# Folding two weight matrices on chip, normalising attention in transposed layout and writing out the order of every engine: linear attention and a multiplicative FFN on one core

## The chip, the cores and the metric

The kernel runs on one core of a Trainium2 chip. A core has five engines with queues of their own: TensorE (PE, with its weight loads PEld), VectorE (DVE), ScalarE (ACT), GpSimd (POOL) and SyncE (SP, which issues the transfers). The metric is device time in microseconds, the median of several runs.

## The reference

```python
def _attn_ref(q, k, v):                      # each (8, 8, 576, 64), f32
    phi = lambda x: np.where(x > 0, x, np.exp(x) - 1.0) + 1.0
    q_p, k_p = phi(q), phi(k)
    kv = np.einsum('bhsd,bhse->bhde', k_p, v)
    z = np.sum(k_p, axis=2)
    num = np.einsum('bhsd,bhde->bhse', q_p, kv)
    den = np.einsum('bhsd,bhd->bhs', q_p, z)[..., None] + 1e-06
    return num / den

def _moe_ref(x, w1, w2, w3, w_out):          # x (4608, 512); w1, w2 (512, 1024)
    a = x @ w1                               # w3 (1024, 1024); w_out (1024, 512)
    b = x @ w2
    h = a * b @ w3                           # (a * b) @ w3
    return h @ w_out

# x is the attention's output, heads side by side: 8 batches x 576 tokens, 8 heads x 64
```

## The kernel before

Two parts share one program. The attention part takes one batch at a time (`attn_load_b`, then `attn_for_b`); the FFN part takes chunks of 512 tokens (`moe_for_chunk`, 9 chunks).

`attn_load_b` loads k, v and q in tiles of 128 tokens (five a batch, the last of 64), all from SP's queue; a tile's piece in memory is 64 floats, 256 bytes. `phi` makes max(x + 1, exp(min(x, 0))) in four steps: two on VectorE from f32 (L80, L82), an Exp on ScalarE (L81), a max on VectorE (L83). v is copied with a column of ones beside each head, so that one product gives both k'v and the sum of k'.

`attn_for_b` forms that product for two heads at a time (kvp, L127), copies its two useful blocks into kvc, and then, for each tile of tokens, transposes q by a matmul with the identity (trp, L146), copies it out (qpT, L153), multiplies by kvc (np, L159), divides in token-major layout on VectorE (L169, L172, L178), transposes the result back (tr, L182) and copies it into xt (L188), the transposed activations of all 4608 tokens.

`moe_for_chunk` forms, for each of eight feature blocks f, a and b (8 matmuls of 512 columns, L201 and L208), copies a out on ScalarE (L215) and multiplies by b on VectorE (L216). Then comes h: for each of eight blocks 8 matmuls with w3 (L222) and a cast on VectorE (L228). Then the output: for each 128 tokens 8 matmuls with w_out (L234), a copy on ScalarE (L241) and a store of 256 KB (L242). A chunk has 64 + 64 + 32 long matmuls.

All weights are loaded by `load_weights`, after the first batch's attention, in 24 pieces through three buffers, each cast to bf16 on VectorE (L59). The source loops over batches, issues the loads of the next batch ahead, and takes an FFN chunk as soon as its tokens are there. The order in which each engine gets its instructions is set by the planner of the language, which weaves attention and FFN work together.

## Time and profile before

| | |
|---|---|
| time, median of 3 runs (range) | 420.39 us (420.13 to 421.15) |
| span of the profiled execution | 417.6 us |
| its own time | not listed apart; the span is 2.8 us under the median |
| TensorE busy | 373.7 us, 89% |
| VectorE busy | 240.5 us, 58% |
| ScalarE busy | 182.0 us, 44% |
| read from and written to memory | 38.8 MB and 9.4 MB |
| granted TensorE clock, mean | 1.000 |

The span runs from the first to the last instruction. The page has the busy time of each engine, the span in 40 slices of 10.4 us with the busy share in tenths, the queues, the chain of work that ended last, and groups of instructions (count, busy time, mean duration in ns, and the idle time just before them). A timeline lists instructions in order: start, length, engine, line, shape, count; in brackets the idle time before and what ended it. A matmul's listed length holds its way through the pipeline, so that what one costs in a row is the distance between starts. Stretches give, for each interval: length, then busy time of PE, PEld, DVE, ACT and POOL with counts, the granted clock, the mean share of the queues and GB/s.

### The profile page before, as it was taken

What the parts mean: (1) busy time and instruction counts of PE and PEld (TensorE: products, weight loads), DVE (VectorE), ACT (ScalarE), POOL (GpSimd) and SP (SyncE); (2) the same over time, 40 slices, a digit from 0 to 9 for tenths busy, and PEclk for the clock granted to TensorE, in tenths of its full rate; (3) what the DMA queues carried; (4) which work ended last, traced back from release to release, by engine and by line L of the source; (5) the groups of instructions that cost most, each with busy time, mean ns of one, the idle gap of its engine ahead of it and who ended that gap; (6) DMA issues with size and microseconds to landing.
All of it is one profiled execution on the core that took longest, in us unless ns stands there. A gap on an engine that the chain in (4) does not pass through costs nothing.

```text
span 417.6 us, 5799 instructions
## 1 busy us (share of the span) xinstructions
PE 373.7 (89%) x2042; PEld 178.1 (43%) x2080; DVE 240.5 (58%) x696; ACT 182.0 (44%) x373; POOL 0.7 (0%) x6
## 2 busy tenths in 40 slices
PE   1054699899999999999999999999999999999996
PEld 0032344344444544454445444544454444444442
DVE  4667678776796698668947871353135313331440
ACT  4565543157755783678348701640164013103202
POOL 0000000000000000000000000000000000000000
PEclk9999999999999999999999999999999999999999
DMA  9998288996993998399639001100110011002002
GB/s 180 201 216 232 80 301 278 260 230 152 187 179 86 224 212 149 86 220 210 116 89 230 14 11 52 48 2 0 53 49 2 0 52 51 0 11 91 2 0 100
DMA packets 121180, 48.61 MB, mean 116 GB/s; under 512 B 113472, under 2 KB 113472, under 8 KB 121152
## 3 DMA queue, kind: packets, MB, share of 16 engines
q1 hardware_dynamic: 121152, 48.25, 52.3%
q8 instruction: 16, 0.26, 0.3%
q14 instruction: 12, 0.10, 0.1%
HBM read 38.80 MB, written 9.44 MB: 115 GB/s over the span
## 4 chain that ended last, share of the span: by engine, by line
PE 77%; ACT 9%; DVE 5%; DMA 4%; SPq 3%; issue 2%; ACTq 0%; DVEq 0%
PE h_ps L222 29%; PE o_ps L234 15%; PE b_ps L208 12%; PE a_ps L201 11%; PE np L159 4%; ACT qpT L153 3%; PE kvp L127 3%; PE tr L182 2%; DMA t<-in_moe_w_dram 2%; ACT xt L188 2%; ACT tmp L81 1%; DMA qt<-in_q_dram 1%; SPq L102 1%; ACT kvc L137 1%; SPq L97 1%
## 5 line engine op out<-in xcount | busy, mean ns | idle before, releaser
L222 PE MATMUL h_ps<-ab_t,w_sb 128*128 128x512 bf16 x565 | 127.9, 379 | 1.8 <-DVE w_sb L59 1.1
L222 PEld LDWEIGHTS <-w_sb 128*128 128x128 bf16 x576 | 55.2, 98 | 66.1 <-DVE w_sb L59 2.0
L201 PE MATMUL a_ps<-xt,w_sb 128*128 128x512 bf16 x273 | 78.1, 385 | 0.4
L208 PE MATMUL b_ps<-xt,w_sb 128*128 128x512 bf16 x282 | 77.6, 380 | 0.6 <-issue 0.2
L228 DVE CAST h_t<-h_ps 128x512 bf16<-128x512 f32 x72 | 49.5, 690 | 42.0 <-PE h_ps L222 40.8
L81 ACT ACTIVATE tmp<-tmp 128x512 bf16<-128x512 bf16 (+1 forms) x80 | 50.3, 633 | 53.0 <-DVE tmp L80 52.7
L216 DVE TENSOR_TENSOR ab_t<-a_sb,b_ps 128x512 bf16<-128x512 f32 x72 | 49.1, 682 | 42.1 <-PE b_ps L208 39.5
L241 ACT COPY o_sb<-o_ps 128x512 f32<-128x512 f32 x36 | 21.1, 585 | 99.4 <-PE o_ps L234 98.8
L234 PE MATMUL o_ps<-wo_sb,h_t 128*128 128x512 bf16 x282 | 63.3, 379 | 0.3
L215 ACT COPY a_sb<-a_ps 128x512 f32<-128x512 f32 x72 | 42.4, 589 | 41.6 <-PE a_ps L201 36.1
L234 PEld LDWEIGHTS <-h_t 128*128 128x128 bf16 x288 | 28.2, 98 | 33.9 <-DVE h_t L228 0.2
L208 PEld LDWEIGHTS <-w_sb 128*128 128x128 bf16 x288 | 26.5, 97 | 26.5 <-issue 1.0
L201 PEld LDWEIGHTS <-w_sb 128*128 128x128 bf16 x288 | 26.9, 99 | 24.5 <-issue 0.8
L188 ACT CAST xt<-tr 128x512 bf16<-128x512 f32 (+1 forms) x40 | 21.7, 542 | 30.5 <-PE tr L182 30.4
L169 DVE TENSOR_SCALAR den<-np 128x4 f32<-128x4 f32 (+1 forms) x80 | 11.4, 160 | 40.7 <-PE np L159 39.9
L127 PE MATMUL kvp<-vt_all,kp_all 128*128 128x130 bf16 (+1 forms) x160 | 19.3, 242 | 17.1 <-ACT vt_all L107 17.1
L178 DVE TENSOR_TENSOR o_t<-np,den 128x256 bf16<-128x256 f32 (+1 forms) x80 | 31.6, 415 | 0.1
L182 PE MATMUL tr<-ident,o_t 128*128 128x128 bf16 (+1 forms) x160 | 22.9, 229 | 9.7 <-DVE o_t L178 9.3
L159 PE MATMUL np<-kvc,qpT 128*128 128x130 bf16 (+1 forms) x160 | 18.9, 240 | 8.5 <-ACT qpT L153 6.0
L182 PEld LDWEIGHTS <-o_t 128*128 128x128 bf16 (+1 forms) x160 | 13.2, 100 | 29.9 <-DVE o_t L178 22.2
L107 ACT CAST vt_all<-vt 128x512 bf16<-128x512 f32 (+1 forms) x40 | 24.6, 614 | 1.6 <-DMA vt<-in_v_dram 1.2
L127 PEld LDWEIGHTS <-kp_all 128*128 128x128 bf16 (+1 forms) x160 | 11.9, 103 | 25.3 <-DVE kp_all L83 17.7
(24 smaller groups left out, 205.5 us busy)
## 6 DMA issues: line engine op xcount, KB each, us to landing
out_dram<-o_sb SPq DMA_DIRECT2D x36, 256.0 KB, 2.0
kt<-in_k_dram SPq DMA_DIRECT2D x32, 256.0 KB, 5.0
vt<-in_v_dram SPq DMA_DIRECT2D x32, 256.0 KB, 5.0
qt<-in_q_dram SPq DMA_DIRECT2D x32, 256.0 KB, 5.1
t<-in_moe_w_dram SPq DMA_DIRECT2D x16, 512.0 KB, 4.6
t<-in_moe_w_out_dram SPq DMA_DIRECT2D x8, 256.0 KB, 3.1
kt<-in_k_dram SPq DMA_DIRECT2D x8, 128.0 KB, 4.8
vt<-in_v_dram SPq DMA_DIRECT2D x8, 128.0 KB, 4.4
```

The lines of the kernel that those rows point to most:

```text
L81: nc.scalar.activation(out=tmp, in_=tmp, func=AF.Exp)
L127: nc.tensor.matmul(kvp[:, a, :], kp_flat[:ssz, st, hp_ * P:(hp_ + 1) * P], vt_flat[:ssz, st, hp_ * (2 * D + 2):(hp_ + 1) * (2 * D + 2)], s ...
L159: nc.tensor.matmul(nps[hp_ // 2][:ssz, hp_ % 2, :], qpT[:, hp_, :ssz], kvc[:, hp_, :], start=(hp_ % 2 == 0), stop=(hp_ % 2 == 1),)
L178: nc.vector.tensor_tensor(out=dst, in0=num_src, in1=rden, op=ALU.mult)
L182: nc.tensor.matmul(tr2[:, hp_, :ssz], o_t[:ssz, hp_ * P:(hp_ + 1) * P], ident[:ssz, :ssz], start=(hp_ == 0), stop=(hp_ == HP - 1),)
L201: nc.tensor.matmul(a_ps[:, :tsz], w1_sb[:, kc, f * P:(f + 1) * P], xt_flat[:, kc * NTOK + tc0: kc * NTOK + tc0 + tsz], start=(kc == 0), st ...
L208: nc.tensor.matmul(b_ps[:, :tsz], w2_sb[:, kc, f * P:(f + 1) * P], xt_flat[:, kc * NTOK + tc0: kc * NTOK + tc0 + tsz], start=(kc == 0), st ...
L215: nc.scalar.copy(out=a_sb[:, :tsz], in_=a_ps[:, :tsz])
L216: nc.vector.tensor_mul(out=ab_t[:, f, :tsz], in0=a_sb[:, :tsz], in1=b_ps[:, :tsz])
L222: nc.tensor.matmul(h_ps[:, :tsz], w3_sb[:, kc, f * P:(f + 1) * P], ab_t[:, kc, :tsz], start=(kc == 0), stop=(kc == FC - 1),)
L228: nc.vector.tensor_copy(out=h_t[:, f, :tsz], in_=h_ps[:, :tsz])
L234: nc.tensor.matmul(o_ps[:msz, :], h_t[:, kc, m0:m0 + msz], wo_sb[:, kc, :], start=(kc == 0), stop=(kc == FC - 1),)
```

## The change

The program is written anew, with these parts.

- *Folding.* w3 @ w_out (1024 x 512) is formed on chip at the start (`wf_unit`, eight times: transpose 128 rows of w3, copy out, eight matmuls with w_out, copy out). The FFN is then (a * b) @ wf: the h stage and its casts are gone.
- *Attention.* phi is max(x + 1, min(exp(x), 1)): Exp on ScalarE straight from the loaded f32, a min in bf16 and one fused add-and-max on VectorE. `kv_unit` writes two masked matrices per pair of heads: k'v, and the sum of k' repeated in 64 columns. With q transposed (`tr_unit`), `nd_unit` gives numerator and denominator of 512 tokens already in transposed layout; the quotient is n * exp(-ln(d + 1e-6)): two activations and a product that writes xt. The second transposition is gone.
- *Token order.* 512 of a batch's 576 tokens are loaded with four consecutive tokens on a partition: pieces of 1 KB, one transfer for 1 MB. The other 64 tokens are loaded with the heads split over two halves of the partitions. xt's columns follow that order, and the output is stored back in the right rows.
- *Order.* The planner is off (`manual_schedule`); each engine gets its instructions in the order of the source. Loads of weights and inputs share one ring of six buffers.

```diff
+    ctx.enter_context(tc.manual_schedule())
+    nc.scalar.preload_act_table_set("natural_log_exp_and_others")
...
+    ld = ctx.enter_context(tc.tile_pool(name="ld", bufs=6))
+    e_p = ctx.enter_context(tc.tile_pool(name="e", bufs=2))
+    mm_ps = ctx.enter_context(tc.tile_pool(name="mm_ps", bufs=4, space=bass.MemoryType.PSUM))
+    at_ps = ctx.enter_context(tc.tile_pool(name="at_ps", bufs=2, space=bass.MemoryType.PSUM))
...
+    def load_qkv(name, src, b):
+        t = ld.tile([P, JW + RW], F32, tag="ld", name=f"{name}32")
+        nc.sync.dma_start(
+            out=t[:, 0:JW].rearrange("p (h x) -> p h x", h=H),
+            in_=src[b, :, 0:NJ * P, :].rearrange("h (p j) d -> p h (j d)", j=NJ),
+        )
+        for hh in range(2):
+            nc.sync.dma_start(
+                out=t[hh * R:(hh + 1) * R, JW:].rearrange("p (h d) -> p h d", d=D),
+                in_=src[b, hh * 4:(hh + 1) * 4, NJ * P:S, :].rearrange("h p d -> p h d"))
...
+    def phi_steps(name, b, dst_j, dst_r):      # JW + RW = 2304 columns
+        def ex(i):
+            s = slice(i * half, (i + 1) * half)
+            nc.scalar.activation(out=e[:, s], in_=x[:, s], func=AF.Exp)
+            nc.vector.tensor_scalar_min(out=e[:, s], in0=e[:, s], scalar1=1.0)
+        def st(j):
...
+            nc.vector.scalar_tensor_tensor(
+                out=dst_j[:, j, :].rearrange("p (h d) -> p h d", h=H),
+                in0=xj, scalar=1.0, in1=ej, op0=ALU.add, op1=ALU.max)
...
+        return [lambda: ex(0), lambda: ex(1), lambda: st(0), lambda: st(1),
+                lambda: st(2), lambda: (st(3), sr())]
...
+    def kv_unit(b):                            # 20 small matmuls into kvp
...
+        nc.vector.tensor_tensor(out=t[:, :, 0, :], in0=src[:, :, :, 0:D], in1=mask, op=ALU.mult)
+        nc.vector.tensor_tensor(out=t[:, :, 1, :],
+            in0=src[:, :, :, D:D + 1].to_broadcast([P, KC, 2, D]), in1=mask, op=ALU.mult)
...
+    def tr_unit(b, part):                      # 8, 8, 4 transposes; a copy on VectorE each
...
+    def nd_finish(n_ap, d_ap, dst, shape):
+        r = lr.tile(shape, F32, tag="lr", name="r")
+        nc.scalar.activation(out=r, in_=d_ap, func=AF.Ln, bias=eps[:, 0:1])
+        nc.scalar.activation(out=r, in_=r, func=AF.Exp, scale=-1.0)
+        nc.vector.tensor_tensor(out=dst, in0=n_ap, in1=r, op=ALU.mult)
+    def nd_unit(b, hp):                        # 2 matmuls of 512; ndr_unit: 8 of 64
+        for i in (1, 0):
+            nc.tensor.matmul(nd[:, i, :], t[:, hp, i, :], qt[:, hp, 0:NJ * P], ...)
...
+    def f_unit(c, f):                          # a and b as before, ACT copy, DVE product
+    def o_unit(c, m):                          # 8 matmuls with wf_sb, ACT copy, store
...
+    def wf_unit(i, w3b):
+        tp = at_ps.tile([P, FC, P], BF16, tag="at", name="w3p")
+        for kc in range(FC):
+            nc.tensor.transpose(tp[:, kc, :], w3b[:, kc * P:(kc + 1) * P], ident)
+        w3t = setup.tile([P, FC, P], BF16, tag="w3t", name="w3t")
+        nc.scalar.copy(out=w3t, in_=tp)
+        ps = mm_ps.tile([P, DM], F32, tag="mm", name="wf_ps")
+        for kc in range(FC):
+            nc.tensor.matmul(ps, w3t[:, kc, :], wo_sb[:, kc, :], ...)
+        nc.scalar.copy(out=wf_sb[:, i, :], in_=ps)
...
+    w3r[0] = load_w(moe_w3, 0, 2, 0, DFF)      # the start
+    wo_a = load_w(moe_w_out, 0, 4, 0, DM)
+    wo_b = load_w(moe_w_out, 4, 8, 0, DM)
+    w3r[1] = load_w(moe_w3, 2, 4, 0, DFF)
+    load_qkv("k", k, 0)
+    w3r[2] = load_w(moe_w3, 4, 6, 0, DFF)
+    t0 = cast_w3(0)
+    for x in range(4):
+        nc.gpsimd.tensor_copy(out=wo_sb[:, x, :], in_=wo_a[:, x, :])
+    load_qkv("v", v, 0)
+    ...                                        # wo_b's casts: POOL and VectorE in turn
+    w3r[3] = load_w(moe_w3, 6, 8, 0, DFF)
+    load_qkv("q", q, 0)
+    wf_unit(0, t0[:, 0, :])
+    wf_unit(1, t0[:, 1, :])
+    t1 = cast_w3(1)
+    wf_unit(2, t1[:, 0, :])
+    ks = k_steps(0)
+    run(ks[:2])
+    wf_unit(3, t1[:, 1, :])
+    run(ks[2:])
+    ...                                        # wf_unit 4, v_steps(0), 5, 6
+    wr = [load_w(moe_w1, 0, KC, 0, 512), load_w(moe_w2, 0, KC, 0, 512)]
+    run(q_steps(0))
+    wf_unit(7, t3[:, 1, :])
+    ...                                        # kv_unit(0), tr_unit x3, nd_unit x4, ndr_unit
+    ...                                        # loads: w1, w2 second halves, k, v of batch 1
+    cast_w(0)
+    cast_w(1)
+    load_qkv("q", q, 1)
+    ...                                        # f_unit(0, 0..2), cast_w(2), cast_w(3), f_unit(0, 3)
+    for f in range(4, FC):
+        f_unit(0, f)
+        run(prep[2 * (f - 4):2 * (f - 3)])     # k and v steps of batch 1
+    prep = q_steps(1)
+
+    for c in range(1, n_chunks + 1):           # n_chunks = 9
+        if c == 1:
+            run(prep)
+            kv_unit(1)
+            for p in range(3):
+                tr_unit(1, p)
+            for m in range(4):
+                o_unit(0, m)
+                nd_unit(1, m)
+            ndr_unit(1)
+            for n, s in (("k", k), ("v", v), ("q", q)):
+                load_qkv(n, s, 2)
+            run(k_steps(2) + v_steps(2) + q_steps(2))
...
+        a = c + 1                              # has: a < 8
+        if has and a + 1 < B:                  # loads of batch a + 1
...
+            units = [F(0), KV, F(1), O(0), T(0), T(1), F(2), T(2), O(1), F(3), N(0), F(4), N(1),
+                     O(2), F(5), N(2), F(6), N(3), NR, O(3), F(7)]
...
+        for i, u in enumerate(units):          # O: chunk c - 1; none at c = 1
+            u()
+            if has and a + 1 < B:              # 14 steps of batch a + 1, from unit 7 on
+                if i == 7:
+                    pq = k_steps(a + 1) + v_steps(a + 1) + q_steps(a + 1)
+                if i >= 7:
+                    run(pq[:2] if i > 7 else pq[:1])
+                    del pq[:2 if i > 7 else 1]
```

F, KV, T, N, NR and O stand for `f_unit`, `kv_unit`, `tr_unit`, `nd_unit`, `ndr_unit` and `o_unit`. In chunks 7 and 8 there is no attention; chunk 8's four `o_unit`s end the program. P is 128, R is 64, NJ is 4.

## The prediction

> **What bounds the kernel now.** I read the page's busy times and slices first, then the groups by line and shape, then stretches and the order of instructions.

> ```profile
> PE 373.7 (89%) x2042; PEld 178.1 (43%) x2080; DVE 240.5 (58%) x696; ACT 182.0 (44%) x373; POOL 0.7 (0%) x6
> PE   1054699899999999999999999999999999999996
> DMA  9998288996993998399639001100110011002002
> q1 hardware_dynamic: 121152, 48.25, 52.3%
> L222 PE MATMUL h_ps<-ab_t,w_sb 128*128 128x512 bf16 x565 | 127.9, 379 | 1.8 <-DVE w_sb L59 1.1
> ```

> TensorE is busy from slice 5 (about 55 us) to the end: after the start it is the bound, and h_ps alone is a third of it. The other engines and the queues have room. Before 55 us TensorE waits. What one instruction costs is the distance to the next in an unbroken row:

> ```profile
> 54.76 0.63 PE L208 MATMUL b_ps<-xt,w_sb 128*128 128x512 bf16 x1
> 55.18 1.49 PE L201 MATMUL a_ps<-xt,w_sb 128*128 128x512 bf16 x3
> 57.10 0.39 PE L146 MATMUL trp<-ident,qp_all 128*128 128x128 bf16 x4
> 54.35 0.62 PE L159 MATMUL np<-kvc,qpT 128*128 128x130 bf16 x4 [0.31 <-ACT qpT L153]
> ...
> 58.81 0.41 PE L159 MATMUL np<-kvc,qpT 128*128 128x130 bf16 x4
> 59.27 0.38 PE L208 MATMUL b_ps<-xt,w_sb 128*128 128x512 bf16 x1
> ```
> ```profile
> 95.86 1.03 PE L201 MATMUL a_ps<-xt,w_sb 128*128 128x512 bf16 x4
> ```

> A 512-column matmul takes (1.49-0.63)/2 = 0.43 us at 55 us and (1.03-0.38)/3 = 0.217 us at 96 us: TensorE runs at half pace through the sparse start and at full pace once its work is dense. A small matmul is about 0.06 us at full pace ((0.41-0.22)/3), 0.13 us slow.

> ```profile
> 77.11 0.42 DVE L80 TENSOR_SCALAR tmp<-kt 128x512 bf16<-128x512 f32 x1
> 77.44 0.42 DVE L59 CAST wo_sb<-t 128x512 bf16<-128x512 f32 x1
> ...
> 83.51 0.68 DVE L228 CAST h_t<-h_ps 128x512 bf16<-128x512 f32 x1
> 84.11 0.42 DVE L80 TENSOR_SCALAR tmp<-qt 128x512 bf16<-128x512 f32 x1
> ```

> VectorE follows at 0.335 us for 512 columns from SBUF and 0.60 us from PSUM, some 0.085 us below the durations.

> ```profile
> L59 DVE CAST w_sb<-t 128x1024 bf16<-128x1024 f32 x16 | 10.8, 684 | 3.2 <-DMA t<-in_moe_w_dram 3.2
> L83 DVE TENSOR_TENSOR kp_all<-kp_all,tmp 128x512 bf16<-128x512 bf16 x32 | 13.4, 420 | 4.0 <-ACT tmp L81 3.6
> L178 DVE TENSOR_TENSOR o_t<-np,den 128x256 bf16<-128x256 f32 x64 | 25.3, 418 | 0.1
> L216 DVE TENSOR_TENSOR ab_t<-a_sb,b_ps 128x512 bf16<-128x512 f32 x72 | 49.1, 682 | 42.1 <-PE b_ps L208 39.5 <-PE a_ps L201 1.0 <-PE tr L182 0.9
> L81 ACT ACTIVATE tmp<-tmp 128x512 bf16<-128x512 bf16 x64 | 40.3, 634 | 43.5 <-DVE tmp L80 43.3
> L153 ACT CAST qpT<-trp 128x512 bf16<-128x512 f32 x32 | 18.9, 589 | 1.3 <-PE trp L146 1.2
> L153 ACT CAST qpT<-trp 128x256 bf16<-128x256 f32 x8 | 3.0, 378 | 0.0
> L81 ACT ACT_TABLE_LOAD x1 | 1.3, 1283 | 0.7 <-PEq L280 0.7
> masks.py:199 POOL TENSOR_SCALAR_AFFINE_SELECT ident<-ident 128x128 bf16<-128x128 bf16 x1 | 0.3, 292 | 0.1
> ```
> ```profile
> 20.00:25.00 5.00, 2.89 (x18) 1.46 (x18) 3.07 (x16) 3.66 (x13) 0.00 (x0) 1.00 1.35 218
> ...
> 50.00:55.00 5.00, 4.00 (x23) 1.89 (x22) 3.28 (x11) 2.55 (x5) 0.00 (x0) 1.00 0.86 314
> ```
> ```profile
> 4.16 0.43 DVE L80 TENSOR_SCALAR tmp<-kt 128x512 bf16<-128x512 f32 x1 [2.40 <-DMA kt<-in_k_dram]
> ```

> Slopes: ScalarE 0.83 ns per column (589 and 378), VectorE 0.51 ns from SBUF (684 against 422) and 1.04 ns from PSUM (682 against 418). Queues: 218 GB/s in q/k/v's 256 B pieces, 314 in the weights' long rows (at 0.86 share); the first load reaches VectorE at 4.2 us. Both 5-us rows have clock 1.00 where the half pace stands, so I read the pace from the distances.

> **The change, part by part.**
> *TensorE.* Per 512 tokens the h stage (64 matmuls) goes: 160 become 96 x 0.217 = 20.8 us. The fold costs 64 transposes and 64 matmuls once. Attention per batch: 20 (kv) + 20 (transposes) + 8 (ndr) small ones, 2.9 us, and 8 x 0.217 = 1.7 us (nd): 4.6 us. A full chunk is 25.4 us. Steady TensorE work falls by 9 x 13.9 = 125 us.

> *VectorE.* Per batch, phi of k and q: two mins over 1152 columns (0.335 + 640 x 0.51 ns = 0.66 us), four fused add-and-max over 512 columns, one over 256. That fused form isn't in the trace: bounds 0.335 (L83, all bf16) and 0.60 (L216, which like it reads f32); I take 0.60. That is 8.1 us for both. v 1.4 us, kvz 2 x 0.60, transposed q 2 x 1.15 + 0.34 us, nd's products 4 x 0.60 + 0.34 us: 16 us. With eight products of f_unit 20.9 us a chunk, under TensorE's 25.4. h_t's casts (49.5 us) go. [...]

> *ScalarE.* Twelve evacuations at 0.59, four Exps over 1152 columns (0.634 + 640 x 0.83 ns = 1.16 us), ten Ln or Exp at about 0.63: 18.0 us a chunk, beside TensorE. If that cover went, it would be the bound only above 25.4.

> *Queues.* The bytes stay (48 MB). A chunk moves 3.54 MB in and 1.05 MB out: at 218 GB/s 21 us, hidden. 1 KB pieces lie between 218 and 314; I take 280. Order on SP's queue matters at two places: v of batch 0 waits for w3's first casts (about 8 us, early enough), and batch 2's loads are queued behind the output of o_unit(0,3).

> **The sum**, stage by stage in the new order of issue:
> 1. *To f_unit(0,0).* w3's first part and w_out, 3.15 MB at 314, land at 13 us; POOL's casts of w_out (between 0.42 as on VectorE and 4 x 0.29, take 1.0) let the fold start at 15. Each unit is a chain: 8 matmuls 1.73, ScalarE's two copies 0.59 + 1.01 (w3t is 1024 columns), 0.17 of hand-over: 3.5 us. Seven and a last 1.73 end at 41.2; the Exps of k and of q sit in ScalarE's order between fold copies, 2.3 each: 45.8; half pace for three of the eight units (start, and the gap at q) 3 x 1.7: 51. The q loads (9.8 MB) have landed by 38-48 and are covered; the fold chain is late, not the loads. Then kv slow 2.6, kvz 1.3, transposes out 2.6: 57.4. nd: first unit 2.7 (matmuls, Ln, Exp, product), the next three 1.35 apart on ScalarE, ndr 0.95, the first weight cast 0.34: **65**. Bounds: 56 (no half pace) to 72 (half pace throughout).
> 2. *Chunk 0's f_units:* 8 x 1.73 + 1.7 for restarting slow = 15.5: **81**.
> 3. *Until f_unit(1,0)'s product.* VectorE: product, v, q phi: 87; kvz and the first transposed q: 89.7. Four (o_unit + nd) 2.17 apart, 1.7 slow: o_unit(0,3) ends at 99.6. Only then SP issues batch 2: 100.6 + 2.2 + 3.54 MB/280 = 115.4 for q, and q's two Exps, min and fused steps (5.7) stand ahead of the product: **121**. Bounds -3 (350 GB/s), +4 (218).
> 4. *Rest of chunk 1:* VectorE's 20.9 bounds, of which 0.9 after TensorE's end: **141**.
> 5. *Chunks 2-5.* 25.4 each, plus a stall: the phi steps for the next batch are issued between f_unit 3 and 5, 10 us of TensorE for some 13 us of VectorE; so nd(2)'s product is late and ndr waits for that PSUM buffer. Between 0 and 3.5; near the middle, 1.7: 27.1 x 4 = 108.4: **249.5**.
> 6. *The rest.* Chunk 6 (no phi) 25.5, chunks 7 and 8 20.8 each, the last o_units 6.9: **323.5**.

> ```profile
> 406.78 7.07 PE L234 MATMUL o_ps<-wo_sb,h_t 128*128 128x512 bf16 x31
> ...
> 413.93 0.59 ACT L241 COPY o_sb<-o_ps 128x512 f32<-128x512 f32 x1 [1.19 <-PE o_ps L234]
> ```

> The end after the last matmul stays, 417.6 - 413.9 = 3.7: span 327.2. Runs stand 2.8 us over the span (420.4, the median, against 417.6): **330 us**.

> **Half pace.** The rows say slow before 56 us and full from 57 on. [...] It speaks against this change, whose start and chunk change leave TensorE waiting.

> **Rivals.**
> - *Better overlap.* No chunk stall (-6.8), fused steps at 0.335 (about -6), little half pace (-7), loads at 350 (-3): 308 or less. For it: VectorE is at 82% of a chunk. Against: all have to come together. 1 in 10.
> - *VectorE becomes the bound.* If the fused step, which reads 64-column pieces apart, costs 1.2 us, phi grows by 4.8 a batch and a chunk is VectorE's 25.7 plus its waits, about 29. Stages 1, 3 and 4 give 12, four chunks 8: 350. Nothing in the trace shows such a form. 1 in 10.
> - *Table loads.* If Ln and Exp lay in different tables, each unit would pay 2 x 1.28: 12.8 in stage 1, 7 in stage 3, and ScalarE's 30.8 would bound chunks 1-6 (29): 378. The change loads one table by name for both. 3 in 100.
> - *Loads bind.* At 150 GB/s stage 3 grows by 11, each chunk is 4.59 MB/150 = 30.6: some 360. It decides under 4.59/27.1 = 169 GB/s; the trace's slowest pieces do 218. 4 in 100.
> - *Slower than before.* One mechanism: TensorE stays at half pace in the chunks. 928 long matmuls x 0.213 = 198: over 500. It decides when some 420 stay slow (90/0.213). Against it: at 25.4 of 27.1 us TensorE is as dense as the rows at 96 us. 1 in 100.

> That folding brings nothing is no rival: the slices show no other engine near 330 us of work.

> **How the numbers follow.** The forecast has 72 in 100: 330, own range 309-346 from the bounds of stages 1 (-9, +7), 3 (-3, +4) and 5 (-7, +7), not all at once. With VectorE's case the range is 308-352 and leaves about 18 in 100 out. The runs before spread by 0.24%, so 0.3% is about what can be told from no change. All cases but the last are faster: 0.98; same 0.01; slower 0.01.

> **What would show it.** Right: TensorE dense from about 65 us; fold units 3.5 us apart with ScalarE's w3t copy ahead of each; a hole before f_unit(1,0)'s product ended by the load of q; chunks of 27 us; no h_ps. Wrong: chunks at 29 or more with VectorE without gaps, several table loads, fold units of 5 us, or a hole that ends much earlier because loads or VectorE are quicker than priced.

## The result: 344 us, ratio 0.817, and the profile after

The changed kernel takes 344.4 us (median of 4 runs, 340.4 to 348.3) against 420.3 us for the kernel before on the same chip: a ratio of 0.8166, 95% interval 0.8119 to 0.8212. The forecast was 330 us with a range of 308 to 352. The profiled execution took 344.31 us, span 342.5. Medians here are over all runs, and the ratios leave out runs more than 1.5% above the fastest of the same kernel, so that a ratio can lie under the quotient of two medians.

The page after (busy times, then the span in 40 slices of 8.6 us: TensorE's busy tenths, the granted clock):

```profile
PE 278.5 (81%) x1440; PEld 128.6 (38%) x1440; DVE 172.8 (50%) x306; ACT 155.2 (45%) x237; POOL 12.5 (4%) x26
PE   1747484986962894998899699969988999999995
PEclk9989865795886797899699989989998999999999
```

TensorE lost 95 us of busy time, and VectorE, the next, is busy for half the span. What is new is how uneven TensorE's row is: holes up to slice 13, then a dip in every third or fourth slice, and the granted clock dips beside them (mean 0.893, before 1.000). The waits of TensorE (total, times, longest, in us) say which:

```profile
PE nd L248 <- DVE xt L232: 18.1, 6, 3.8
PE wf_ps L298 <- ACT w3t L295: 12.3, 7, 3.2
PE kvp L182 <- DVE vt L163: 10.4, 4, 7.5
```

The first is the stall of ndr in chunks 1 to 5 (3.84, then four times 3.34, and 0.93 at the start), the second the fold's chain, the third mostly the wait for batch 2's v (its 7.5), whose loads and phi come late. All three had been named. By the forecast's six stages, from the order of TensorE's instructions:

| stage | forecast | measured | difference |
|---|---|---|---|
| 1. f_unit(0,0) starts | 65 | 59.7 | -5.3 |
| 2. length of chunk 0's f_units | 16 | 16.2 | +0.2 |
| 3. from there to f_unit(1,0)'s product | 40 | 40.0 | 0 |
| 4. rest of chunk 1 | 20 | 22.0 | +2.0 |
| 5. chunks 2-5 | 108.4 | 126.1 | **+17.7** |
| 6. chunk 6; 7 and 8; last o_units | 25.5; 41.6; 6.9 | 26.0; 41.4; 6.9 | +0.3 |
| end after the last matmul; time over span | 3.7; 2.8 | 4.2; 1.8 | -0.5 |

One term carries the miss of 14 us: the four chunks. Here is chunk 2's end and chunk 3's, in the order of TensorE's instructions:

```profile
164.38 0.59 PE L248 MATMUL nd<-qt,kvz 128*128 128x64 bf16 x8 [3.34 <-DVE xt L232]
164.78 3.60 PE L275 MATMUL o_ps<-wf_sb,ab 128*128 128x512 bf16 x8
168.18 1.91 PE L265 MATMUL a_ps<-xt,w_sb 128*128 128x512 bf16 x4
170.97 1.03 PE L265 MATMUL a_ps<-xt,w_sb 128*128 128x512 bf16 x4
...
196.60 0.39 PE L248 MATMUL nd<-qt,kvz 128*128 128x64 bf16 x8 [3.34 <-DVE xt L232]
196.83 2.83 PE L275 MATMUL o_ps<-wf_sb,ab 128*128 128x512 bf16 x8
199.46 1.81 PE L265 MATMUL a_ps<-xt,w_sb 128*128 128x512 bf16 x4
201.10 1.03 PE L265 MATMUL b_ps<-xt,w_sb 128*128 128x512 bf16 x4
201.97 1.03 PE L265 MATMUL a_ps<-xt,w_sb 128*128 128x512 bf16 x4
```

The stall is 3.34 us, not 1.7. And behind it the o_unit's eight matmuls start (168.18-164.78)/8 = 0.425 us apart instead of 0.217: half pace. From ndr to the next chunk's first matmul lie 0.23 + 1.73 + 0.865 + 0.865 = 3.69 us of work at full pace; chunk 2 takes 170.97-164.38 = 6.59, chunk 3 201.97-196.60 = 5.37, chunks 4 and 5 the same 5.37. So half pace costs 2.9 us once and 1.68 three times, and another 0.83 at the start of chunk 2.

Why the stall is 3.34 is seen in VectorE's order ahead of it (all engines, the same stretch):

```profile
159.65 0.63 ACT L231 ACTIVATE r<-r 128x512 f32<-128x512 f32 x1
...
160.30 1.90 DVE L133 SCALAR_TENSOR_TENSOR qj<-q,e 128x512 bf16<-128x512 f32 x3
...
162.11 0.68 DVE L269 TENSOR_TENSOR ab<-a_sb,b_ps 128x512 bf16<-128x512 f32 x1
162.71 0.69 DVE L133 SCALAR_TENSOR_TENSOR qj<-q,e 128x512 bf16<-128x512 f32 x1
163.31 0.42 DVE L138 SCALAR_TENSOR_TENSOR qr<-q,e 128x256 bf16<-128x256 f32 x1
163.65 0.69 DVE L232 TENSOR_TENSOR xt<-nd,r 128x512 bf16<-128x512 f32 x1
```

The reciprocal of nd(2) is ready at 159.65 + 0.63 = 160.28. Its product on VectorE, which frees the PSUM buffer that ndr needs, starts at 163.65: it stands in order behind four fused steps and qr of the *next* batch's phi and one f product, 3.37 us.

### The profile page after: what moved, and what is told of

Read it like the earlier page. It is cut to its first block, busy times and chain, and to the rows that moved or that the text cites. A ratio compares the mean times of both kernels' runs of the same rounds, so it can differ in the third digit from the quotient of the medians.

```text
span 342.5 us, 3960 instructions
## 1 busy us (share of the span) xinstructions
PE 278.5 (81%) x1440; PEld 128.6 (38%) x1440; DVE 172.8 (50%) x306; ACT 155.2 (45%) x237; POOL 12.5 (4%) x26
## 4 chain that ended last, share of the span: by engine, by line
PE 74%; DVE 11%; ACT 6%; DMA 5%; issue 3%; SPq 0%; DVEq 0%; ACTq 0%
PE o_ps L275 20%; PE a_ps L265 19%; PE b_ps L265 18%; PE wf_ps L298 5%; PE nd L238 3%; PE kvp L182 3%; DVE qj L133 3%; DMA w<-in_moe_w_out_dram 3%; PE tp L211 2%; ACT w3t L295 2%; DMA k<-in_k_dram 2%; ACT e L127 2%; DVE xt L232 2%; PE kvp L188 1%; DVE ab L269 1%
## 5 line engine op out<-in xcount | busy, mean ns | idle before, releaser
L265 PEld LDWEIGHTS <-w_sb 128*128 128x128 bf16 x576 | 58.1, 103 | 77.9 <-issue 17.0
L269 DVE TENSOR_TENSOR ab<-a_sb,b_ps 128x512 bf16<-128x512 f32 x72 | 49.2, 684 | 75.4 <-PE b_ps L265 75.4
L275 PE MATMUL o_ps<-wf_sb,ab 128*128 128x512 bf16 x288 | 74.5, 408 | 0.0
L275 PEld LDWEIGHTS <-ab 128*128 128x128 bf16 x288 | 28.7, 103 | 35.4 <-issue 6.5
L230 ACT ACTIVATE r<-nd,eps 128x512 f32<-128x512 f32 (+1 forms) x40 | 25.7, 644 | 23.5 <-PE nd L248 13.0
L232 DVE TENSOR_TENSOR xt<-nd,r 128x512 bf16<-128x512 f32 (+1 forms) x40 | 25.3, 633 | 19.7 <-ACT r L231 19.5
L231 ACT ACTIVATE r<-r 128x512 f32<-128x512 f32 (+1 forms) x40 | 23.5, 587 | 1.3
L182 PE MATMUL kvp<-vt,kj 128*128 128x130 bf16 x128 | 15.5, 251 | 10.4 <-DVE vt L163 10.4
L238 PE MATMUL nd<-qt,kvz 128*128 128x512 bf16 x64 | 20.5, 409 | 2.9 <-DVE xt L232 2.3
L133 DVE SCALAR_TENSOR_TENSOR qj<-q,e 128x512 bf16<-128x512 f32 x32 | 21.6, 724 | 0.3
L133 DVE SCALAR_TENSOR_TENSOR kj<-k,e 128x512 bf16<-128x512 f32 x32 | 20.9, 685 | 0.2
L248 PE MATMUL nd<-qt,kvz 128*128 128x64 bf16 x64 | 3.7, 209 | 18.2 <-DVE xt L232 18.1
L182 PEld LDWEIGHTS <-kj 128*128 128x128 bf16 x128 | 9.2, 109 | 15.9 <-DVE vt L163 8.4
```

The costliest lines, as they stand in the source:

```text
L133: nc.vector.scalar_tensor_tensor(out=dst_j[:, j, :].rearrange("p (h d) -> p h d", h=H), in0=xj, scalar=1.0, in1=ej, op0=ALU.add, op1=ALU.max)
L182: nc.tensor.matmul(o, kj[:, j, hp * P:(hp + 1) * P], vt[:, j, 2 * hp:2 * hp + 2, :].rearrange("p h e -> p (h e)"), start=(j == 0), stop=False)
L230: nc.scalar.activation(out=r, in_=d_ap, func=AF.Ln, bias=eps[:, 0:1])
L231: nc.scalar.activation(out=r, in_=r, func=AF.Exp, scale=-1.0)
L232: nc.vector.tensor_tensor(out=dst, in0=n_ap, in1=r, op=ALU.mult)
L238: nc.tensor.matmul(nd[:, i, :], t[:, hp, i, :], qt[:, hp, 0:NJ * P], start=True, stop=True)
```

## The experiments

Each kernel is the changed one with the edit shown (shortened where there are dots or comments), unless it says otherwise; ratios are to the kernel before, run on the same chip.

**One phi step per unit.** The first question is whether the order of the phi steps makes the stall and the half pace.

```diff
-                    run(pq[:2] if i > 7 else pq[:1])
-                    del pq[:2 if i > 7 else 1]
+                    run(pq[:1])
+                    del pq[:1]
```

> The 14 phi and v steps of the next batch are issued one per unit (units 7 to 20) instead of two (units 7 to 14); nothing else changes. Theory A (in chunks 1 to 5 ndr's matmuls wait 3.3 us for nd(2)'s product, which stands behind those steps on VectorE, and the pause costs another 1.7 us of half pace behind it): the wait ndr <- xt goes from 18 us to under 3, chunks 3 to 5 go from 31.0 to about 26 us, the time from 344 to about 321. Theory B (VectorE's sum of work bounds the chunks): moving it changes nothing, 340 to 344. Theory C (the half pace comes from dense work itself, a power limit, and not from the pause): the wait goes but the half pace stays, about 330.

Measured 320.3 us (319.5 to 323.9), ratio 0.764 [0.7589, 0.7691]: 24 us less. TensorE's wait, and chunk 1's ndr, the longest pause left:

```profile
PE nd L248 <- DVE xt L232: 2.8, 2, 1.8
```
```profile
131.29 0.39 PE L248 MATMUL nd<-qt,kvz 128*128 128x64 bf16 x8 [1.85 <-DVE xt L232]
131.51 1.03 PE L265 MATMUL a_ps<-xt,w_sb 128*128 128x512 bf16 x4
```

18.1 us of waiting became 2.8, and from chunk 2's ndr on the next ones follow 27.1 and 26.0 us later. Behind the 1.85 us pause the matmuls are 0.217 apart: no half pace.

**Stall or half pace?** To separate the two, TensorE gets matmuls whose result nobody reads just ahead of ndr, so that the stall stays and the pause goes: 16, then 8.

```diff
+    def warm(n):
+        d = mm_ps.tile([P, NCH], F32, tag="mm", name="warm")
+        for _ in range(n):
+            nc.tensor.matmul(d, wf_sb[:, 0, 0:P], wf_sb[:, 0, :], start=True, stop=True)
...
-        NR = lambda: ndr_unit(a)
+        NR = lambda: (warm(16) if a + 1 < B else None, ndr_unit(a))
```

> Sixteen long matmuls whose result nobody reads are put ahead of ndr in chunks 1 to 5, 3.5 us of TensorE work in the 3.3 us pause; the order of all else stays. Theory A: the pause stays filled, o_unit and f_unit behind it run at 0.217 us a matmul, each of five chunks loses its 1.7 us or more of half pace: about 334 to 336. Theory C: half pace stays, or grows, 344 or more. If the dummies cost more than they warm: 345 or more.

> Eight long matmuls instead of sixteen whose result nobody reads ahead of ndr in chunks 1 to 5: 1.7 us of the pause stay filled, 1.6 us stay empty. If the half pace needs an idle time of about 3.4 us: as with sixteen, 333 to 335. If any pause of over a us brings it: as without, 340 to 344.

Measured 332.9 us (332.1 to 339.0), 0.7909 [0.7888, 0.7931], with 16, and 333.8 us (332.0 to 336.7), 0.7968 [0.7929, 0.8007], with 8. Chunk 2 with 16, then chunk 2 with 8, in the order of TensorE's instructions:

```profile
164.23 0.39 PE L248 MATMUL nd<-qt,kvz 128*128 128x64 bf16 x8
164.46 1.89 PE L280 MATMUL o_ps<-wf_sb,ab 128*128 128x512 bf16 x8
```
```profile
160.00 0.39 PE L248 MATMUL nd<-qt,kvz 128*128 128x64 bf16 x8 [1.61 <-DVE xt L232]
160.23 1.89 PE L280 MATMUL o_ps<-wf_sb,ab 128*128 128x512 bf16 x8
```

Made to do work that nobody reads, the kernel is 11.5 us faster; the o_unit behind runs at full pace, and a pause of 1.61 us left open does no harm. The stall itself stays: from chunk 3's ndr to chunk 4's it is 29.32 us in both runs (222.87-193.55 and 218.64-189.32) against 31.00 after, and the difference is the 1.68 of half pace. The sum from the rows after is near the 11.5: 8.8 us in chunks 2 to 5 (above: 2.9 + 0.83 + 3 x 1.68) and 1.8 in chunk 1 behind its stall. Of the 24 us that the spread steps gave, about 11 are half pace, 13 the stall of four chunks (4 x 3.34 = 13.4) and 2 that of chunk 1 (3.84-1.85); two new waits of 0.91 us take some of it back.

**Batch 2's loads earlier.** The hole of stage 3: ScalarE's rows show the Exps of batch 2 waiting for their loads, which SP issues only behind o_unit(0,3)'s output.

```profile
103.02 2.22 ACT L127 ACTIVATE e<-k 128x1152 bf16<-128x1152 f32 x2 [5.14 <-DMA k<-in_k_dram]
110.45 2.22 ACT L127 ACTIVATE e<-q 128x1152 bf16<-128x1152 f32 x2 [5.22 <-DMA q<-in_q_dram]
```

```diff
     cast_w(3)
+    for n, s in (("k", k), ("v", v), ("q", q)):
+        load_qkv(n, s, 2)
...
-            for n, s in (("k", k), ("v", v), ("q", q)):
-                load_qkv(n, s, 2)
             run(k_steps(2) + v_steps(2) + q_steps(2))
```

> Batch 2's loads are issued right behind the weight casts in chunk 0 instead of behind the output of o_unit(0,3). Theory A (f_unit(1,0)'s product waits for the phi steps of batch 2, and these for its loads, k landing at 103 us): k's Exp starts at about 98, the product comes at about 107 to 108 instead of 116: time about 335 to 336. Rival (VectorE's queue alone holds it, the loads are hidden): no change, 344.

Measured 334.6 us (331.9 to 337.1), 0.7942 [0.7896, 0.7988]: 10 us less. ScalarE's same two rows:

```profile
100.69 2.20 ACT L127 ACTIVATE e<-k 128x1152 bf16<-128x1152 f32 x2
102.80 2.20 ACT L127 ACTIVATE e<-q 128x1152 bf16<-128x1152 f32 x2
```

The wait for the transfers is gone, and q's Exps follow k's at once.

**The fold as a pipeline.** The fold units are 3.5 us apart though TensorE works 2.2 us in each. Split each: transposes and copy of unit i + 1 ahead of the matmuls of unit i, and put the Exps of phi behind the fold's copies.

```diff
-    wf_unit(i, ...)
+    wf_a(i + 1, ...)                  # transposes, copy out
+    wf_b(i)                           # matmuls, copy out
```

> The fold is pipelined: the transposes and the copy of unit i+1 are issued ahead of the matmuls of unit i, and the Exps of k and q stand behind the fold copies instead of between them. Theory A (the start is bound by the chain transpose, ScalarE copy, matmul, 3.5 us a unit with two holes of 3.3 us): units 2.2 to 2.5 us apart, the last fold matmul at about 33 us instead of 45, f_unit(0,0) at 48 to 50 instead of 59.7, time about 333. Rival (the loads of w3, k, v and q bound the start): f_unit(0,0) moves by 3 us or less, 341 or more.

Measured 340.5 us (338.8 to 342.1), 0.8104 [0.8067, 0.814]: a miss. The units come 2.2 us apart while they are fed, but then TensorE waits:

```profile
32.35 1.03 PE L295 MATMUL w3p<-ident,w3b 128*128 128x128 bf16 x8 [5.99 <-DVE w3b L323]
```

w3's last cast stood behind k's and v's steps on VectorE, in the order that I had written. In the next version that cast goes ahead of v's steps, and k's steps ahead of the fifth unit's transposes.

> The pipelined fold again, with w3's last cast ahead of v's casts and k's phi issued ahead of fold unit 4. In the run before it the fold units were 2.2 us apart, but the last two waited 6 us for w3's last cast, which stood behind k's and v's steps on VectorE. Theory A (the chain of the fold, then q's phi, bounds the start): no hole over 3 us in the fold, last fold matmul at 33 to 35 us instead of 40.5, f_unit(0,0) at 48 to 50 instead of 56.8, time about 332 to 335. Rival (loads: w3's last part, w1 and w2 come no earlier than about 45): f_unit(0,0) at 54 or later, 339 or more.

Measured 336.6 us (335.1 to 337.2), 0.8007 [0.7984, 0.803], a little short of what was expected. f_unit(0,0) starts at 51.59 instead of 59.66, where 48 to 50 had been expected. The eight units are done near 34 instead of 45; then q's phi and kvz lead on VectorE:

```profile
40.98 1.04 PE L211 MATMUL tp<-ident,qj 128*128 128x128 bf16 x8 [2.75 <-DVE kvz L197]
```

**All mendings of the order together.** Spread steps, early loads (here behind chunk 0's last f_unit), the piped fold, q's phi of batch 1 woven into chunk 0, phi of batch 2 woven between the o and nd units of chunk 1. A second version also puts kv_unit(1) behind f_unit(0,5) and two steps fewer ahead of ndr's product.

```diff
     f_unit(0, 0)
+    prep = k_steps(1) + v_steps(1) + q_steps(1)      # was: q's steps in chunk 1
+    for f in range(1, FC):
+        f_unit(0, f)
+        ...
+        run(prep[2 * (f - 1):2 * f])                 # second version: kv_unit(1) after f = 5
...
+            pq = k_steps(2) + v_steps(2) + q_steps(2)
+            run(pq[:4])
             for m in range(4):
                 o_unit(0, m)
                 nd_unit(1, m)
+                run(pq[4 + 2 * m:6 + 2 * m])         # second version: not for m = 3
             ndr_unit(1)
-            run(k_steps(2) + v_steps(2) + q_steps(2))
+            run(pq[12:])
```

> All together: phi steps one per unit, batch 2's loads issued in chunk 0, the pipelined fold, q's phi of batch 1 woven into chunk 0's f_units, and phi of batch 2 woven between the o_units and nd_units ahead of chunk 1. Theory A: -24 (spread, measured), -10 (loads, measured), -10 (fold), and about -9 for the two woven phis (the pauses of 2.5 and 7.5 us ahead of kv_unit in the trace of the changed kernel): about 291, between 286 and 300. Rival (the gains share one slack, so that the woven work only moves the wait to the next engine): 305 or more.

> All the order edits, and two more at the change from chunk 0 to chunk 1: kv_unit(1) is issued behind f_unit(0,5) instead of behind chunk 0, and two fewer phi steps of batch 2 stand ahead of ndr's product. Theory A (the waits of 2.9 us ahead of the second transposed q and of 5.0 us ahead of f_unit(1,0) in the run with all edits come from these orders): 294 to 297. Rival (they only move): 300.

Measured 299.95 us (299.2 to 300.8), 0.7141 [0.7123, 0.7159], and 299.0 us (298.93 to 299.48), 0.7123 [0.7112, 0.7134]: 45 us under the changed kernel, where 53 had been added up. The second version gained nothing that the intervals separate, as its rival had it: a_ps's wait for ndr's product fell from 6.8 to 5.8 us in all. What is left are waits for VectorE at the start and around chunk 1.

**The fold alone.** The kernel before, with its planner, its loads and its attention; only the fold is formed on chip after the weights, and the h stage goes.

```diff
+            fold()                    # eight times: transposes, copy, 8 matmuls, copy
...
-        h_t = moe_sb.tile([P, FC, NCHUNK], BF16, tag="h_t")
-        ...                           # 64 matmuls and eight casts a chunk
...
-                    h_t[:, kc, m0:m0 + msz],
-                    wo_sb[:, kc, :],
+                    ab_t[:, kc, m0:m0 + msz],
+                    wf_sb[:, kc, :],
```

> The fold alone in the kernel before: w3 @ w_out formed on chip after the weights, no h stage; attention, loads, token order and the planner's order stay. Theory D (the fold carries most of the gain; TensorE loses 9 x 13.9 = 125 us and gains 64 transposes and 64 matmuls, 17.5): TensorE would be about 265 us of work behind the same start, 320 to 335 us in all. Rival E (without the h stage's cover the old attention is late next: VectorE has 240.5 - 49.5 = 191 us and ScalarE about 195, and the chain transpose, copy, product, divide, transpose, copy runs per 128 tokens): TensorE waits in the chunks, 345 to 380.

Measured 340.4 us (338.8 to 341.2), 0.8098 [0.8073, 0.8123]: as fast as the whole change. TensorE's busy tenths, in slices of 8.5 us:

```profile
PE   1134455325878999999999999899999999999995
```

TensorE is thin for ten slices and dense from the fourteenth on, without the dips of the changed kernel. The time lies between the two expectations: TensorE is not held up in the chunks, as rival E had it, but the start is not the same either, since the fold waits 13.9 us in six pieces for VectorE's casts of w_out (the longest 10.2).

**The old token order.** Pieces of 256 B as before, four transfers a tensor; the output rows follow.

```diff
-            in_=src[b, :, 0:NJ * P, :].rearrange("h (p j) d -> p h (j d)", j=NJ),
+            in_=src[b, :, j * P:(j + 1) * P, :].rearrange("h p d -> p h d"),   # j = 0..3
```

> The changed kernel with the old token order: q, k and v come in 256-byte pieces (four transfers of 128 tokens a tensor instead of one), the output rows follow; all else stays. Theory G (the 1 KB pieces pay only where a load is waited for: the start, behind the fold, hardly; batch 2's hole before chunk 1, 3.54 MB at 218 instead of about 350 GB/s, 6 us): 348 to 354. Rival (the pieces matter in every chunk, since a chunk's loads then take 16 of its 31 us): 360 or more. Rival (all loads are hidden): 344.

Measured 347.3 us (343.2 to 349.5), 0.8204 [0.8164, 0.8244], against 0.8166 [0.8119, 0.8212]: not separated. The throughput in slices, of this kernel and then of the changed one:

```profile
GB/s 267 349 266 255 324 323 228 51 1 0 81 195 218 215 238 225 201 32 31 33 234 252 54 95 222 192 31 184 227 129 31 33 32 61 34 61 31 63 61 123
```
```profile
GB/s 267 398 356 380 373 154 124 2 2 0 61 225 363 325 298 94 3 61 31 41 324 142 33 146 330 34 30 265 243 31 31 33 31 61 33 62 32 63 61 122
```

The loads around chunk 1 run at 195 to 238 GB/s (slices 12 to 17) instead of 298 to 363 (13 to 15), and the times are not separated: at most some 5 us (0.8244 - 0.8119 = 0.0125 of 420). That does not show that the pieces cost nothing. In this trace q's Exps of batch 2 wait 8.02 us for their load instead of 5.22, and from f_unit(0,0) to chunk 1's ndr it is 79.1 us (137.96-58.88) instead of 74.5 (134.12-59.66): 4.6 us lost, near theory G's 6. Behind it most of that comes back, largely because chunk 2's pause, as long as before, is this time followed by full pace:

```profile
137.96 0.45 PE L249 MATMUL nd<-qt,kvz 128*128 128x64 bf16 x8 [4.06 <-DVE xt L233]
...
167.24 0.39 PE L249 MATMUL nd<-qt,kvz 128*128 128x64 bf16 x8 [3.34 <-DVE xt L233]
167.68 1.67 PE L276 MATMUL o_ps<-wf_sb,ab 128*128 128x512 bf16 x7
169.19 1.03 PE L266 MATMUL a_ps<-xt,w_sb 128*128 128x512 bf16 x4
```

The seven matmuls are (169.19-167.68)/7 = 0.216 us apart. From chunk 1's ndr to chunk 3's it is 58.6 us here (196.56-137.96) and 62.5 after (196.60-134.12).

**The planner's order.** The changed kernel with one line less: each engine then gets its instructions in the planner's order, from the same source.

```diff
-    ctx.enter_context(tc.manual_schedule())
```

> The changed kernel with the planner of the language on again, which may move each engine's instructions; the source's units stay. Theory F (the hand-written order is what holds the changed kernel at 344: the phi steps ahead of nd(2)'s product, batch 2's loads behind the output, the serial fold): an order that takes what is ready avoids some of it, 315 to 335. Rival (the planner weaves no better than the hand): 340 to 360.

> The kernel with all the order edits (300 us) with the planner on. If the planner is the better order: under 297. If it is no better than a mended hand-written order: 300 to 315. It tells whether what is left above TensorE's own work (some 240 us) is order, or waits that no order removes.

Measured 288.4 us (287.5 to 289.4), 0.6872 [0.6849, 0.6895], and, with the source of the mended order under the planner, 286.7 us (285.4 to 288.4), 0.683 [0.6802, 0.6858]. Neither theory expected the first. Its slices of TensorE, of 7.2 us, and its waits for the product ahead of ndr:

```profile
PE   0875865999789979999999999999999999999994
```
```profile
PE nd L247 <- DVE xt L231: 2.5, 2, 2.1
```

The 56 us can be placed by ndr's start in each chunk. In chunk 2 it is at 164.38 after and at 125.70 here: 38.7 us are gained by then. From there to chunk 5's ndr it is 94.2 us after (258.61) and 78.3 here (203.97): 16.0 more, and 1.7 of half pace behind chunk 5's stall: 56.3, the difference of the spans (342.5-286.2). Stretches of 50 us show the first part, after and then the planner's (length, busy PE, PEld, DVE, ACT, POOL with counts, clock, DMA share, GB/s):

```profile
50.00:100.00 50.00, 38.88 (x179) 17.21 (x178) 26.50 (x51) 22.74 (x36) 0.00 (x0) 0.75 0.20 64
100.00:150.00 50.00, 36.24 (x195) 16.61 (x193) 33.09 (x61) 22.16 (x31) 0.00 (x0) 0.81 0.67 207
```
```profile
50.00:100.00 50.00, 46.78 (x263) 21.81 (x267) 41.94 (x79) 34.36 (x51) 0.00 (x0) 0.96 0.68 219
100.00:150.00 50.00, 47.87 (x282) 23.47 (x286) 42.46 (x80) 35.05 (x55) 0.00 (x0) 1.00 0.68 206
```

From 50 to 100 us the planner keeps the queues at 0.68 where the hand-written order has 0.20, and VectorE at 41.94 us where that has 26.50: loads and phi of the next batches run beside chunk 0, and TensorE issues 263 matmuls instead of 179. That these two are what it gains there is read from the rows; the piped fold, the early loads and the spread steps one by one (above) agree with it, but the planner's choices were not undone one at a time.

## Why the forecast held, and its one mis-sized term

*Right, in part by luck.* Faster, and inside the range, with the stages' mechanisms as told, but for the half pace inside the chunks: fold units 3.5 us apart; a hole before f_unit(1,0)'s product ended by q's load; a stall of ndr behind the phi steps in each chunk; one table load; transfers hidden in the later chunks (ScalarE's Exps wait for loads only around chunk 1, 5.14 and 5.22 us). The rows for the first (TensorE, after):

```profile
15.18 1.90 PE L298 MATMUL wf_ps<-wo_sb,w3t 128*128 128x512 bf16 x8 [1.15 <-ACT w3t L295]
...
18.69 1.90 PE L298 MATMUL wf_ps<-wo_sb,w3t 128*128 128x512 bf16 x8 [1.16 <-ACT w3t L295]
...
24.29 3.20 PE L298 MATMUL wf_ps<-wo_sb,w3t 128*128 128x512 bf16 x8 [3.25 <-ACT w3t L295]
...
41.74 3.59 PE L298 MATMUL wf_ps<-wo_sb,w3t 128*128 128x512 bf16 x8 [3.25 <-ACT w3t L295]
```

Three units came at half pace for most of their matmuls, as the sum had it: the first (its last four matmuls, from 11.83 to 13.42, 0.40 us apart), and the two behind the Exps of k and of q (24.29 to 27.35 and 41.74 to 45.12, eight each, 0.38 and 0.42). How long half pace lasts behind a wait is shown by no run of before: the 1.7 us that stages 1 to 3 take for it each time were an estimate, eight matmuls 0.213 us slower. After, it cost 27.35-24.29-1.73 = 1.33 us and 1.65 us in these two units, and 64.64-59.66-3 x 0.865 = 2.39 us where chunk 0's f_units start.

The number held better than the sum. Stage 5 went 17.7 us over, outside its own bounds of -7 and +7, and stage 1's 5.3 us hid part of that. Without them the time would have been some 350, just under the range's 352, and that end of the range came from a rival that did not occur (VectorE as the bound); the forecast's own range ended at 346. The sign of being right "chunks of 27 us" did not come: chunk 2 took 33.1 us, chunks 3 to 5 31.0 each. VectorE did not bind them: it has a gap of 4.85 us behind chunk 2's stall and of 3.83 behind the next two, and the spread steps took the stall away with VectorE's work unchanged.

*Mis-sized: stage 5.* The forecast gave each chunk 25.4 us of work and a stall "between 0 and 3.5; near the middle, 1.7". The middle was a choice with no row behind it. The rows that it had would have given more: five pieces of VectorE work, priced at 0.60, and qr at 0.34 stand in order between the reciprocal and the product: 3.3 us. Measured are 26.0 of work (+0.6 x 4), 3.34 of stall (+1.64 x 4), and half pace, 2.9 + 0.83 + 3 x 1.68 = 8.8, which stood in the forecast as a risk of the start and of the chunk change, but in no chunk's term: 2.4 + 6.6 + 8.8 = 17.8. The two warm-up runs show the last part, the spread steps the sum.

*Stage 1 came 5 us early.* The fold began at 9.33 and not 15. Groups by line and shape after (count, busy us, mean ns, idle before):

```profile
L128 DVE TENSOR_SCALAR e<-e 128x1152 bf16<-128x1152 bf16 x32 | 14.4, 454 | 36.9 <-ACT e L127 36.8
L213 DVE COPY qt<-tp 128x1024 bf16<-128x1024 bf16 x16 | 10.5, 685 | 7.7 <-PE tp L211 7.6
L133 DVE SCALAR_TENSOR_TENSOR kj<-k,e 128x512 bf16<-128x512 f32 x32 | 20.9, 685 | 0.2
L323 POOL CAST wo_sb<-w 128x512 bf16<-128x512 f32 x4 | 2.3, 615 | 5.8 <-DMA w<-in_moe_w_out_dram 5.8
L76 ACT ACT_TABLE_LOAD x1 | 1.3, 1283 | 0.7 <-PEq L440 0.7
```

In the second to fifth slice the loads came at 356 to 398 GB/s (the slices above; 267 in the first, which holds the start) where 314 was taken, and GpSimd's first four casts took 0.6 us each, not 1.0. The transposed q was taken as 1.15 a copy and took 0.685. The fused step is 0.685 a duration, the 0.60 apart that was taken: the rival in which VectorE binds (1.2) fell with that. The one of the tables fell with the single load in the last row, and the one of the loads with 298 to 363 GB/s, over the 169 from which it would decide. The min is 0.454 us a duration, an estimated 0.37 apart (0.085 less, as VectorE's rows of before stand); the forecast's slope gave 0.66.

*What the change is worth.* The fold alone gives 80 us. The rest (attention, loads) with the planner's order takes the kernel from 340 to 288, and the hand-written order gives 56 us back, all of that and more. So the TensorE work that the fold takes away, the forecast's main cause, is enough by itself for the whole measured gain, and the order was worth less than nothing. How much of the 52 us is attention, loads or the fold's place at the start was not separated.

## What to carry to other kernels

Before an engine's order is written by hand, time the same source with the planner's order: here that one line is worth 56 us, and mending the hand order step by step won back 45. Where an order is written by hand, list for each product that frees a PSUM buffer what stands ahead of it in its engine's queue, and price the list; "near the middle" is no price. A pause of TensorE can cost twice: itself, and half pace behind it (here, behind 3.34 us, 1.7 us in three chunks, 2.9 in one, and nothing in one chunk of another run); unread matmuls in the pause took the second price away at no cost in time.

## What the runs showed of the hardware

From the distances, the moment at which TensorE's pace changed can be placed inside a row: chunk 3's o_unit takes 199.46-196.83 = 2.63 us for eight matmuls of 0.217 or 0.427, so 3.7 of them are fast and the pace falls at 197.64. In the row behind it four take 201.10-199.46 = 1.64 us, so 3.7 are slow and full pace is back at 201.03, 3.39 us after the fall. For chunks 4 and 5:

```profile
227.83 3.11 PE L275 MATMUL o_ps<-wf_sb,ab 128*128 128x512 bf16 x8
230.73 1.54 PE L265 MATMUL a_ps<-xt,w_sb 128*128 128x512 bf16 x4
...
258.83 3.38 PE L275 MATMUL o_ps<-wf_sb,ab 128*128 128x512 bf16 x8
262.01 1.26 PE L265 MATMUL a_ps<-xt,w_sb 128*128 128x512 bf16 x4
```

The length of the pause does not decide alone. Pauses ahead of ndr of 1.61, 1.85 and 2.12 us (the last in the run with eight unread matmuls, chunk 1) were followed by full pace, and so was one of 3.34 us, in chunk 2 of the old token order, where the same 3.34 us cost 2.9 and three times 1.68 us in the changed kernel. What decides between these was not shown. It may also be why the changed kernel's runs spread over 8 us and those of the last mended order, where chunks 2 to 5 have no such pause, over 0.6; that was not tested.
